# Keys and values of batches 1 to 3 loaded by heads, and a written place for every operation

## The chip, the cores and the metric

One core of a Trainium2 chip runs the kernel. The metric is the device time of one execution in microseconds; the medians are over three runs. A profiled execution leaves a trace, from which all rows below come.

## The reference

Causal attention with a memory term feeds a two-layer network; the attention's output for a token is that token's input row.

```python
# attention: B, H, S, D = 4, 8, 576, 64
scores = q @ k^T / sqrt(D), causal; a = softmax(scores)
local = a @ v
q_p = phi(q)                       # elu(q) + 1
mem_out = (q_p @ M_prev) / (q_p . z_prev + 1e-6)
g = sigmoid(beta)                  # one per head
attn = g * mem_out + (1 - g) * local
# network: 2304 tokens, 512 -> 2048 -> 512
h = x @ w_in                       # x: attn, heads side by side
y = (relu(h) + alpha * min(h, 0)) @ w_out
```

## The kernel before

**Tiling.** Each batch's 576 rows are cut into a first block of 64 and four blocks of 128. The first blocks of all four batches make a fifth set, Z, done first. Attention goes by units (batch, head, pair of blocks [1, 2] or [3, 4]); the two-layer network runs on groups of 256 tokens, in eight steps j of two 128-wide slices of the 2048. Matmuls in reduced width use pairs of f16 tiles, a high and a low part, in three products; batch 0's first pair of blocks and Z use f32.

**Tiles and phases.** `load_batch(b)` loads q, z, K (tile `kn`) and V with M_prev (tile `vn`); there is one buffer of `kn` and one of `vn`. `kn` is [partition, head, block, 64]: block i's row p of every head lies in partition p. `prep_qk` squares all of `kn` for a scale and `prep_v` takes the maximum over `vn`; `build_qk` and `build_v` split one pair of heads into f16 parts (`k<-kn`, `v<-vn`), and `build_qk` turns them by DMA transposes (`qT<-q`, `k<-k`) and copies halves (`qS<-qT`). `unit_scores` makes scores `s`, `unit_probs` the probabilities `P` and their transpose `PT<-P`, `pair_values` the products in PSUM tile `bank`, written to `xn` and transposed to `x` (`x<-xn`). `moe_in` makes `h` and `gg`, `moe_out` makes `y` and stores. At the start the weights are loaded as f64 words and converted on DVE (`to_f32`, phases C0 to C3).

**Order.** No instruction is issued while the kernel is described. `Work.add` records each with its engine, its phase name (such as `L3k` for loads of batch 3's K, `P21` for probabilities of batch 2, blocks [1, 2]) and the earlier ones whose cells it touches. `Work.issue` then gives each a rank, and `Work.lay` walks a model of the engines in time: whenever an engine is free, it takes the ready operation with the lowest rank. The order of the starts so found is the order of issue; each engine works through its own in sequence. All DMAs, loads and transposes alike, go through SP's queue. The ranks before come from three stages of `STAGES`: shifts in us by phase, or by phase and engine, added to the starts of the stage before.

Of the kernel before, what the change touches and what calls it, by code (L numbers as in the profile page):

```python
# [31 lines left out]
STAGES = [  # L32
    (2, {
        "A0": 10.6, "A:DVE": 50.6, "BK0": 102.5, "BK:ACT": -27.7, "BK:PE": 3.4, "C0": -56.4, "C1": 22.3, "C2": 335.8,
        "C3": -920, "C:ACT": 1096.2, "C:DVE": -3.8, "C:PE": -943.6, "I": -699.2, "I:DVE": 79.2, "I:POOL": 497.7,
        "J:ACT": 470.6, "J:DVE": 108, "J:PE": -179.3, "K": 47.5, "K:POOL": 2.3, "L0K": -713.8, "L0K:DMA": 228.2,
# [6 lines left out]
        "LW:DMA": 605.3, "LZ": 27.3, "LZ:DMA": -1145.9, "Lz": 8.5, "Lz:DMA": -8.6, "N": 87.9, "N:PE": 292.5,  # L43
        "P01": 4, "P03": 3.7, "P11": 777.2, "P13": 823.4, "P21": 168.1, "P23": 236.6, "P31": -675.3, "P33": -247.2,
        "P:ACT": 988.7, "P:DMA": 668.5, "P:DVE": -882.6, "P:PE": -157.8, "S0": 4737.2, "S1": -1253, "S3": -2953.6,
        "S:ACT": -87.5, "S:DVE": 168.1, "V0": -874.8, "V:DVE": 211.2, "V:PE": -90.8, "a0": 5.7, "a1": 46.8,
        "a2": -161.5, "a3": 389.6, "a4": -42.9, "a:ACT": -265.2, "a:DVE": 239.4, "bk0": -173.5, "bk1": 344.8,
        "bk2": 244.5, "bk3": 3.1, "bk:ACT": -687.5, "bk:DMA": 246.9, "bk:DVE": 1380.7, "bk:PE": 100.3, "bv0": -0.7,
# [5 lines left out]
        "o31": 144.8, "o33": 10.1, "o:ACT": -779.8, "o:DMA": 580.1, "o:DVE": -613.6, "o:PE": 33.3, "oZ": 10.8,  # L54
# [5 lines left out]
        "v:DVE": 634.9, "v:PE": 331.4, "x0": -121.5, "x:ACT": 2.1, "x:DVE": 73.7, "y0_10": -412.5, "y0_11": -68.6,  # L60
        "y0_30": 187.3, "y0_31": 1834.4, "y1_10": -18.1, "y1_11": 103.3, "y1_30": -419.6, "y1_31": 103.8,
        "y2_10": 184.2, "y2_11": 220.2, "y2_30": -3073.8, "y2_31": -122.6, "y3_10": 764.1, "y3_11": 98,
        "y3_31": 447.3, "y4_11": -1599.1, "y:ACT": -1231.1, "y:DMA": 642.8, "y:DVE": -750.7, "y:PE": 1282.7,
    }),
# [4 lines left out]
        "C3:PE": -8.9, "C:ACT": 13.2, "C:DVE": 9.3, "C:PE": -17.2, "I": -57.9, "I:POOL": -8.6, "J:ACT": -18.7,  # L69
# [6 lines left out]
        "LW3": -8.7, "LW3:DMA": -22.1, "LW:DMA": -2.8, "LZ:DMA": -42.6, "Lz:DMA": -4.4, "N": 0.9, "N:PE": -13.7,  # L76
# [5 lines left out]
        "P33:DMA": -3.8, "P33:DVE": -7.4, "P33:POOL": -37, "P:ACT": 15, "P:DMA": -20.1, "P:DVE": 8.9, "P:PE": -86.4,  # L82
# [126 lines left out]
        "y:PE": 143.8,  # L209
    }),  # L210
]
WINDOW = 3413.0
RING, SHARE = 1200, 0.95
# [36 lines left out]
class Work:  # L250
# [79 lines left out]
    def price(self, kind, name, outs, ins, kw):  # L330

        o = outs[0]
# [126 lines left out]
    def issue(self, tc):  # L459
        ops = self.ops  # L460
# [1067 lines left out]
```

## Time and profile before

| | |
|---|---|
| median of 3 runs | 563.89 us (560.77 to 564.72) |
| profiled execution | 563.66 us, span 561.9 us |
| mean granted TensorE clock | 0.982 |
| TensorE busy | 536.4 us (95%), 4421 matmuls |
| DVE busy | 450.9 us (80%) |
| ACT busy | 376.7 us (67%) |
| GpSimd busy | 82.8 us (15%) |
| DMA | 82.84 MB, 226026 packets, 216224 of them under 512 bytes |

PE is TensorE's matmul, PEld its weight load, DVE VectorE, ACT ScalarE, POOL GpSimd and SPq the queue of SyncE, on which a DMA's duration is that of its issue. Times are in us from the start of the span. [...] All instructions show line 487, the one that issues them, so groups go by tile: `out<-in`. Matmuls are pipelined and their ends are modelled, so that short gaps between them don't show.

### The profile page before, as it was taken

To read this page: it belongs to the slowest core of one execution; us is meant where nothing else is said; L and a number is where in the kernel's file an instruction comes from. 1 tells how busy PE (TensorE), PEld (TensorE's weight loads), DVE (VectorE), ACT (ScalarE), POOL (GpSimd) and SP (SyncE) were. 2 spreads that over 40 slices of the span, in tenths; PEclk is the share of its full clock that TensorE was granted. 3 is DMA by queue.
4 is the path that set the end of the run, shared out by engine and by line. 5 is a ranking of instruction groups with operands and counts; after the bars stand their busy time and mean duration, and the time that the engine had idled before them with its cause. 6 is when DMAs were issued, how large, how long until landed. Compare 5 with 4: busy or idle time off the path is not lost. (4 is left out here: it accounts for less than half of the span.)

```text
span 561.9 us, 11984 instructions
## 1 busy us (share of the span) xinstructions
PE 536.4 (95%) x4421; PEld 353.5 (63%) x4421; DVE 450.9 (80%) x1197; ACT 376.7 (67%) x790; POOL 82.8 (15%) x142
## 2 busy tenths in 40 slices
PE   9749999999999899999998999999999999999997
PEld 3448654556557566658555766578578765866663
DVE  4989999999999799999897999998679974233232
ACT  2568996778998369978785787796579873232222
POOL 3000510031220012221222110431112110000000
PEclk9869999999999999999998999999999999999999
DMA  8998595836359997579999816799446963000000
GB/s 283 239 353 202 155 238 173 244 94 153 89 127 184 214 231 170 101 140 210 194 201 198 175 34 146 160 232 178 58 118 111 167 138 88 12 11 2 37 1 37
DMA packets 226026, 82.84 MB, mean 147 GB/s; under 512 B 216224, under 2 KB 216240, under 8 KB 225968
## 3 DMA queue, kind: packets, MB, share of 16 engines
q1 hardware_dynamic: 225968, 82.09, 64.5%
q8 instruction: 34, 0.56, 0.4%
q14 instruction: 24, 0.20, 0.1%
HBM read 35.66 MB, written 5.77 MB: 74 GB/s over the span
## 5 line engine op out<-in xcount | busy, mean ns | idle before, releaser
L487 PE MATMUL h<-x,R 128*128 128x256 f16 x1536 | 246.7, 273 | 1.9 <-DMA x<-xn 1.4
L487 PE MATMUL y<-R,gg 128*128 128x512 f16 (+1 forms) x832 | 247.0, 399 | 0.8 <-ACT k L487 0.6
L487 PE MATMUL bank<-v,PT 128*128 128x64 f16 x1224 | 182.1, 193 | 5.3 <-DMA PT<-P 4.5
L487 PEld LDWEIGHTS <-R 128*128 128x128 f16 x1536 | 148.6, 98 | 36.9 <-issue 6.5
L487 PEld LDWEIGHTS <-gg 128*128 128x128 f16 x768 | 74.4, 98 | 78.3 <-DVE gg L487 1.8
L487 PEld LDWEIGHTS <-PT 128*128 128x128 f16 x1224 | 114.4, 98 | 13.6 <-DMA PT<-P 6.9
L487 POOL TENSOR_SCALAR E<-q,nrm,sm 128x64 f32<-128x64 f32 x112 | 67.9, 618 | 310.9 <-DVE sm L487 269.8
L487 ACT ACTIVATE E<-E,mx 128x320 f32<-128x320 f32 (+3 forms) x136 | 81.1, 602 | 21.5 <-DVE mx L487 17.4
L487 DVE SCALAR_TENSOR_TENSOR P<-E,mx,P 128x384 f16<-128x384 f32 (+2 forms) x112 | 75.3, 699 | 8.5 <-ACT P L487 8.4
L487 ACT ACTIVATE P<-E,mx 128x384 f16<-128x384 f32 (+2 forms) x112 | 71.0, 675 | 15.8 <-POOL E L487 12.0
L487 DVE SCALAR_TENSOR_TENSOR r<-r,oma,h 128x256 f32<-128x256 f32 x128 | 56.6, 475 | 20.2 <-ACT r L487 20.0
L487 DVE SCALAR_TENSOR_TENSOR gg<-r,gsc,gg 128x512 f16<-128x512 f32 x56 | 41.8, 748 | 36.5 <-ACT gg L487 35.0
L487 ACT ACTIVATE r<-h 128x512 f32<-128x512 f32 x72 | 42.3, 589 | 35.8 <-PE h L487 23.9
L487 ACT ACTIVATE gg<-r,gsc 128x512 f16<-128x512 f32 x56 | 40.1, 717 | 37.4 <-PE y L487 33.4
L487 DVE CUSTOM_DVE_ANT_0 E<-s,mask,pm 128x320 f32<-128x320 f32 (+2 forms) x96 | 56.9, 608 | 7.6 <-PE s L487 7.5
L487 PE MATMUL s<-k,qT 128*128 128x64 f16 (+5 forms) x136 | 37.9, 294 | 1.3 <-DMA k<-k 1.3
L487 PE MATMUL s<-k,qS 128*128 128x192 f16 (+4 forms) x120 | 34.0, 294 | 0.0
L487 PE MATMUL h<-R 128*128 128x256 f32 x128 | 32.7, 383 | 0.0
L487 PEld LDWEIGHTS h<-R 128*128 128x128 f32 x128 | 22.3, 192 | 6.6 <-issue 3.0
L487 ACT ACTIVATION_READ_ACCUMULATOR E<-E,mx 128x1 f32 x124 | 23.5, 189 | 0.0
L487 ACT ACTIVATE xn<-bank,xsc 128x256 f16<-128x256 f32 x28 | 12.9, 462 | 12.3 <-PE bank L487 12.3
L487 DVE SCALAR_TENSOR_TENSOR xn<-bank,xsc,xn 128x256 f16<-128x256 f32 x28 | 13.4, 480 | 9.4 <-ACT xn L487 9.4
(183 smaller groups left out, 636.7 us busy)
## 6 DMA issues: line engine op xcount, KB each, us to landing
q<-in_q_dram SPq DMA_DIRECT2D x16, 256.0 KB, 4.3
vn<-in_v_dram SPq DMA_DIRECT2D x16, 256.0 KB, 5.2
out_dram<-t SPq DMA_DIRECT2D x16, 256.0 KB, 2.4
kn<-in_moe_w_in_dram SPq DMA_DIRECT2D x6, 512.0 KB, 6.7
kn<-in_moe_w_out_dram SPq DMA_DIRECT2D x6, 512.0 KB, 5.3
kn<-in_k_dram SPq DMA_DIRECT2D x12, 256.0 KB, 4.0
qS<-qT SPq DMA_DIRECT2D x24, 128.0 KB, 2.6
R<-in_moe_w_in_dram SPq DMA_DIRECT2D x4, 512.0 KB, 5.6
```

The costliest lines, as they stand in the source:

```text
L487: fn(*a, **kw)
```

## The change

In batches 1 to 3, K's four blocks of 128 rows were loaded by four DMAs, each with all heads (256 KB), and so were V's. Now each of the eight heads has one DMA that fills its four blocks (128 KB). The loads of the first 64 rows and of M_prev stay as they were, and so does batch 0.

`STAGES` and the code that applies it are gone. A table `PLAN` has for each phase and engine the places of its operations in the order in which they are recorded, in steps of 0.1 us, each written as the difference from the one before (`"L3k:DMA": "3792 -1014 -243 ..."` stands for 379.2, 277.8, 253.5 us and so on). One walk of `lay` with these places as ranks gives the order. The prices of DMAs in the walk's model are changed as well; they act on nothing but the order. The first place of `L3k` and of `L3v` belongs to the load of the first 64 rows, the second of `L3v` to M_prev, the other eight to the heads; `Lz` holds four loads of z, then alpha and beta; `LZ` and `LK` load q and K of the set Z.

```diff
-STAGES = [
-    (2, {
...
-]
+PLAN = {
...
+    "C0:DVE": "266 -71 175 -199 -45 66 272 16 -42 -2 -88 -168 195 509 53 -247",
...
+    "L2k:DMA": "1613 310 59 137 -18 -348 366 -10 -351",
...
+    "L2v:DMA": "2338 -399 291 -329 120 -56 -356 365 -45 -341",
...
+    "L3k:DMA": "3792 -1014 -243 -4 8 3 27 94 108",
...
+    "L3v:DMA": "2368 50 -173 128 -104 -158 160 162 -185 19",
...
+    "LK:DMA": "-81 -3 99 44",
...
+    "LW0:DMA": "-536 -16 156 -6 -106 -66 7 27",
...
+    "LZ:DMA": "-4 -36 52 47",
...
+    "Lz:DMA": "81 -42 49 56 -75 -35",
...
+    "P21:DMA": "2538 31 75 213 -255 1050 -92 55",
...
+    "a4:DVE": "-426 248 -21 522",
...
+}
...
         if kind == "DMA":
             kb = n * o.shape[0] * size / 1024
             if "transpose" in name:
-                return (800 + 1.75 * kb if kb > 400 else 1130 + 0.6 * kb), 190 + 3.45 * kb, 1655, -1
+                return (800 + 1.75 * kb, 4.1 * kb, 1700, -1) if kb > 400 else (1130 + 0.6 * kb, 3.78 * kb, 1885, -1)
             run = min(x.ap[-1][1] * (2 if x.dtype == F16 else 4) for x in (o, ins[0]))
             packets = 1024 * kb / min(run, 4096)
             if run < 256:
-                return 500, 0.45 * packets, 1800, packets
+                return 500, 0.45 * packets, 2000, packets
             if run >= 4096:
-                return 400, (2.75 if self.phase in ("LW0", "LW1") else 4.9) * kb, 2000, packets
+                rate, late = {"LW0": (3.2, 2600), "LW1": (2.7, 2450)}.get(self.phase, (3.55, 2150))
+                return 400, rate * kb, late, packets
             if run >= 512:
-                return 540, max(300, 4.06 * kb), 1800, packets
-            return 620, (273 if kb > 200 else 200) + 4.17 * kb, 2100, packets
+                if o.tensor.name in self.fixed:
+                    return 400, 1.4 * kb, 1950, packets
+                return (560, 5.3 * kb, 1765, packets) if kb < 200 else (530, 4 * kb, 1800, packets)
+            return (600, 4.5 * kb, 2050, packets) if kb > 200 else (620, 6 * kb, 2090, packets)
...
-        late = [0.0] * len(ops)
-        hold = [max(op[5], op[8][0]) for op in ops]
-        pe = 0.0
-        for i in reversed(range(len(ops))):
-            took = ops[i][8][0] + ops[i][8][1] if ops[i][0] == "DMA" else hold[i]
-            late[i] = min([late[f] - lag for f, lag in after[i]], default=0.0) - took
-            if ops[i][6]:
-                late[i] = pe = min(late[i], pe - hold[i])
-        rank = late
-        for passes, bias in STAGES:
-            rank = [x + 1e3 * sum(bias.get(k, 0) for k in dict.fromkeys((
-                op[7], op[7].rstrip("0123456789_") + ":" + op[0], op[7] + ":" + op[0]))) for x, op in zip(rank, ops)]
-            for n in range(passes):
-                if n:
-                    back = self.lay(after, before, [-s - h for s, h in zip(start, hold)], True)
-                    rank = [-s - h for s, h in zip(back, hold)]
-                start = self.lay(before, after, rank)
-            rank = start
+        plan = {}
+        for x, steps in PLAN.items():
+            at, ranks = 0, []
+            for step, _, times in (y.partition("*") for y in steps.split()):
+                for _ in range(int(times or 1)):
+                    at += int(step)
+                    ranks.append(100.0 * at)
+            plan[x] = iter(ranks)
+        start = self.lay(before, after, [next(plan[f"{op[7]}:{op[0]}"]) for op in ops])
...
         if b:
+
+            def heads(dst, src):
+                return [(dst[:, h, 1:NS], src[b, h, 64:, :].rearrange("(i p) d -> p i d", p=128)) for h in range(H)]
+
+            todo[1][1:] = heads(kn, k)
+            todo[2][2:] = heads(vn, v)
             todo = [[lambda o=o, i=i, c=c: load(o, i, f"L{b}{c}") for o, i in t] for t, c in zip(todo, "qkv")]
         else:
```

## Rows read from the trace of the kernel before

**Rows 1.** Stages of the span: busy us (instructions) by engine, clock, DMA.
```profile
0.00:20.00 20.00, 18.57 (x74) 7.96 (x74) 12.09 (x25) 5.28 (x9) 4.28 (x13) 1.00 0.96 281
20.00:40.00 20.00, 9.98 (x84) 7.54 (x85) 18.17 (x79) 13.96 (x48) 0.00 (x0) 0.69 1.15 304
...
140.00:260.00 120.00, 116.09 (x1043) 77.44 (x1042) 114.66 (x294) 96.86 (x195) 19.39 (x32) 1.00 0.74 160
260.00:325.00 65.00, 60.35 (x558) 40.71 (x557) 56.88 (x164) 47.23 (x108) 14.46 (x22) 0.97 0.95 187
325.00:555.00 230.00, 229.41 (x2090) 156.69 (x2089) 151.66 (x388) 133.97 (x267) 28.29 (x50) 1.00 0.44 91
...
sum 561.90, PE 536.37 PEld 353.48 DVE 450.91 ACT 376.67 POOL 82.79; mean PE 67.05 PEld 44.19 DVE 56.36 ACT 47.08 POOL 10.35
```

**Rows 2.** Who waited for whom, TensorE, whole span: us, times, longest.
```profile
PE bank L487 <- DMA PT<-P: 4.5, 5, 2.7
PE bank L487 <- DVE stv L487: 3.5, 1, 3.5
```

**Rows 3.** The same, from 260 to 325 us.
```profile
PE bank L487 <- DMA PT<-P: 4.3, 4, 2.7
PE s L487 <- DMA k<-k: 0.4, 1, 0.4
```

**Rows 4.** Timeline, TensorE: start, us, instruction, [idle before it, releaser].
```profile
302.77 0.20 PE L487 MATMUL bank<-v,PT 128*128 128x64 f16 x1 [2.65 <-DMA PT<-P]
```

**Rows 5.** Timeline, SP's queue, from 292 to 312 us.
```profile
292.94 1.16 SPq L487 DMA_DIRECT2D q<-in_q_dram  x2
294.14 2.07 SPq L487 DMA_DIRECT2D kn<-in_k_dram  x2
296.32 5.59 SPq L487 DMA_TRANSPOSE PT<-P  x2
301.97 1.29 SPq L487 DMA_DIRECT2D kn<-in_k_dram  x2
...
305.00 0.68 SPq L487 DMA_DIRECT2D vn<-in_v_dram  x1
...
307.91 3.22 SPq L487 DMA_DIRECT2D vn<-in_v_dram  x4
```

**Rows 6.** Instructions on the tile PT, whole span.
```profile
DMA to landing us min/median/max: 2.9/3.9/6.4
```

**Rows 7.** Instructions on the tile PT, from 293 to 306 us.
```profile
DMA to landing us min/median/max: 3.3/4.8/6.4
```

**Rows 8.** Stages after the stall, columns as in rows 1.
```profile
304.00:306.00 2.00, 2.00 (x10) 0.93 (x8) 0.97 (x4) 0.50 (x2) 0.00 (x0) 0.52 1.24 278
306.00:308.00 2.00, 2.00 (x7) 0.78 (x6) 1.86 (x7) 1.54 (x5) 0.00 (x0) 0.62 0.63 142
```

**Rows 9.** Timeline, DVE: splits of K and V, batches 2 and 3.
```profile
270.56 0.87 DVE L487 SCALAR_TENSOR_TENSOR k<-kn,scr,k 128x640 f16<-128x640 f32 x1
...
299.98 0.74 DVE L487 SCALAR_TENSOR_TENSOR v<-vn,scr,v 128x512 f16<-128x512 f32 x1
...
364.28 0.87 DVE L487 SCALAR_TENSOR_TENSOR k<-kn,scr,k 128x640 f16<-128x640 f32 x1
```

**Rows 10.** Timeline, TensorE, where batch 1 takes over.
```profile
185.86 3.11 PE L487 MATMUL h<-x,R 128*128 128x256 f16 x27 [1.21 <-DMA x<-xn]
...
195.26 0.33 PE L487 MATMUL s<-k,qT 128*128 128x192 f16 x2 [0.94 <-DMA k<-k]
```

**Rows 11.** Timeline, SP's queue, start.
```profile
3.99 2.52 SPq L487 DMA_DIRECT2D q<-in_z_prev_dram  x4
...
12.06 0.66 SPq L487 DMA_DIRECT2D q<-in_q_dram  x1
```

**Rows 12.** Timeline, DVE, start.
```profile
20.35 1.23 DVE L487 SCALAR_TENSOR_TENSOR R<-E,R 128x1024 int32<-128x1024 int32 x1
21.50 0.68 DVE L487 TENSOR_REDUCE stq<-q 128x1 f32<-128x512 f32 x1
```

More of the change, by code (lines that the diff above doesn't have):

```diff
@@ L29 @@
 PN = [1, 1, 1, 1, 1]
-STAGES = [
-    (2, {
-        "A0": 10.6, "A:DVE": 50.6, "BK0": 102.5, "BK:ACT": -27.7, "BK:PE": 3.4, "C0": -56.4, "C1": 22.3, "C2": 335.8,
-        "C3": -920, "C:ACT": 1096.2, "C:DVE": -3.8, "C:PE": -943.6, "I": -699.2, "I:DVE": 79.2, "I:POOL": 497.7,
-        "J:ACT": 470.6, "J:DVE": 108, "J:PE": -179.3, "K": 47.5, "K:POOL": 2.3, "L0K": -713.8, "L0K:DMA": 228.2,
[6 rows of a table removed]
[L43 to L48, printed above, removed]
[5 rows of a table removed]
-        "o31": 144.8, "o33": 10.1, "o:ACT": -779.8, "o:DMA": 580.1, "o:DVE": -613.6, "o:PE": 33.3, "oZ": 10.8,
[5 rows of a table removed]
[L60 to L64, printed above, removed]
[4 rows of a table removed]
-        "C3:PE": -8.9, "C:ACT": 13.2, "C:DVE": 9.3, "C:PE": -17.2, "I": -57.9, "I:POOL": -8.6, "J:ACT": -18.7,
[6 rows of a table removed]
-        "LW3": -8.7, "LW3:DMA": -22.1, "LW:DMA": -2.8, "LZ:DMA": -42.6, "Lz:DMA": -4.4, "N": 0.9, "N:PE": -13.7,
[5 rows of a table removed]
-        "P33:DMA": -3.8, "P33:DVE": -7.4, "P33:POOL": -37, "P:ACT": 15, "P:DMA": -20.1, "P:DVE": 8.9, "P:PE": -86.4,
[21 rows of a table removed]
-        "h4_11:PE": -16.7, "h:ACT": 10, "h:DVE": 8.9, "h:PE": -16.3, "n": -27.5, "n:PE": -9.4, "o01": -15,
[5 rows of a table removed]
-        "o33:DVE": 21.3, "o33:PE": -55.2, "o:ACT": -0.5, "o:DMA": -50.1, "o:DVE": 13.1, "o:PE": -18, "oZ": -97,
[4 rows of a table removed]
-        "q:ACT": 39, "q:DVE": 9.7, "r0:ACT": 0.9, "r0:DVE": 9.9, "r:ACT": 35.7, "r:DVE": 13.6, "s01:ACT": -1.2,
[4 rows of a table removed]
-        "s33:ACT": 1.7, "s33:PE": -49.1, "s:ACT": 12.1, "s:DVE": 8.9, "s:PE": -16.3, "sZ": 8.1, "sZ:ACT": 98.3,
[14 rows of a table removed]
-        "y4_11:PE": -16, "y:ACT": 21.9, "y:DMA": 2.5, "y:DVE": 8.4, "y:PE": -16.3,
-    }),
[4 rows of a table removed]
-        "C3:PE": -26.7, "C:ACT": 47.4, "C:DVE": -22.5, "C:PE": 1, "I:DVE": -32.9, "I:POOL": 4.3, "J": 37.8,
[13 rows of a table removed]
-        "P33:DMA": -13.2, "P33:DVE": -9.1, "P:DMA": -3.5, "P:DVE": -22.3, "P:PE": 0.2, "P:POOL": -11, "S0": 2.9,
[27 rows of a table removed]
-        "o33:PE": 65.8, "o:ACT": 7.4, "o:DMA": -10.7, "o:DVE": -24.8, "o:PE": 144.2, "oZ": -53.6, "oZ:ACT": 8.9,
[9 rows of a table removed]
-        "s33:DVE": -8.2, "s33:PE": 41.6, "s:ACT": -5, "s:DVE": -22.3, "s:PE": 143.8, "sZ": -0.9, "sZ:ACT": 37.5,
[15 rows of a table removed]
-        "y:PE": 143.8,
-    }),
-]
```

562 rows, old and new, of tables (PLAN, STAGES) are left out of this document.

## Prediction

> **What bounds the kernel now.** I read the span cut into stages first, then TensorE's waits, then single instructions around the longest wait. TensorE is busy for 536.37 us of 561.9 [rows 1], so the time can only fall where it idles or runs at the lower clock, and the cut shows where that is. From 325 to 555 us it is busy for 229.41 of 230 us at full clock: nothing is to be had there, whatever the order. From 20 to 40 us it is busy for only 9.98 of 20 us at a granted clock of 0.69. From 140 to 260 us it idles 120 - 116.09 = 3.91 us, from 260 to 325 us 65 - 60.35 = 4.65 us, and the clock of that stage is 0.97. The list of waits says on what: 4.5 us on transposes of the probabilities (PT<-P), which go through SP's queue, 4.3 us of them between 260 and 325 us; the 3.5 us on stv belong to the start [rows 2, 3].
>
> The one stall worth the name ends at 302.77 us: TensorE had waited 2.65 us for a PT tile before its next bank matmul [rows 4]. On SP's queue two q loads and two K loads of batch 3, 1 MB in four DMAs, went out from 292.94 to 296.2 us, and the two PT<-P transposes behind them held SP for 5.59 us [rows 5]. Over the whole kernel a PT tile lands 3.9 us after its issue in the median [rows 6]; of the two issued here one took 6.4 us, the longest of all 56 [rows 7]. The loads ahead cost that transpose 2.5 us, which is the stall. [...]
>
> **The change part by part.** *Removed: four block loads each of K and V for batches 1 to 3, with what they tie together.* A block holds all eight heads, so it may overwrite its slice of kn (or vn), of which there is one buffer, only when the last head pair of the batch before has been split. A head load needs only its own pair. In the trace batch 2's K is split from 270.56 us on and the last of its V until 300.7 [rows 9]; the loads of batch 3 go out from 294.14 to 311.1 [rows 5]. By heads the first K load could leave at 271.5. The new places ask for it: V's pieces of batch 3 stand at 211 to 243 us, K's eight heads at 253 to 278, the PT transposes of batch 2's first half at 254 to 365, so SP takes each piece soon after its pair is free, a few at a time instead of four together. I take the 302 us stall as gone with its clock, 2.65 + 1.72 = 4.4 us, and half of the stage's other waits on transposes (4.3 - 2.65 on PT<-P and 0.4 on k<-k [rows 3], 2.05 together): 1.0. **Term A: -5.4 us**, bounds 0 and -6.4 (4.3 + 0.4 + 1.7).
>
> Where batch 1 takes over, TensorE waits 1.21 us for x<-xn and 0.94 us for k<-k [rows 10]. No K or V load is in flight then; the order of transposes causes it, which the new places also change. **Term B: half, -1.1 us**, bounds 0 and -2.15.
>
> *Added: pieces.* Per batch 16 loads of 128 KB take the place of 8 of 256 KB; bytes and the runs of 256 bytes stay the same. SP is held 0.68 us by a 128 KB load, and 2.07, 1.29 and 3.22 us by the eight large ones [rows 5]: 16 x 0.68 = 10.9 against 6.6, 4.3 us more per batch, 13 us in three. Nobody waits for the loads themselves: the first split of batch 3's K starts at 364.28 us [rows 9]. What hides the 13 us is SP's slack between transposes; one that stands behind a piece is late by 0.68 us. Bounds 0 and +13; I take one piece ahead of one awaited transpose in each batch, nearest to the row of a single load: **term C: +2.0 us**.
>
> [...]
>
> *Moved: everything, by the new table.* The three stages of shifts by phase give way to a place for each operation; the list scheduler takes, of the operations that are ready, the one with the lowest place. One move is certain from the table alone, since these loads wait for nothing: at the start the loads of z, K and Q of the first rows are re-ranked. Before, four z loads leave from 3.99 us and Q's first at 12.06 [rows 11]. Now K stands at -8.4 to 5.9, Q at -4 to 5.9, z at 3.9 to 14.4. z is 4 x 128 KB = 0.52 MB, at the 281 GB/s of the first 20 us [rows 1] 1.9 us of transfer. DVE's first operation on q starts at 21.50 us, behind conversions of weights of 1.23 us each [rows 12], and the waits on stv and on what follows hang on that chain. **Term D: -2.0 us** (z's 1.9, rounded). Bounds: 0, because DVE is busy 18.17 of the 20 us from 20 to 40 [rows 1], and if its whole work and not its order sets when the h matmuls can go, the gain is nil; and -4.4, with the last two conversions (2 x 1.23 us) put behind q as well. From 325 us on: 0, for want of idle time; should the new order starve TensorE, that is in the rivals.
>
> **Sum.** -5.4 - 1.1 + 2.0 - 2.0 = -6.5. The profiled execution took 563.66 us (span 561.9), 0.23 below the median 563.89, a difference that I leave out. Forecast 557.2 us, 1.2% below the median.
>
> **Rivals.** *Larger.* The new places fit the whole order better, not only the loads: every idle microsecond of 140 to 325 us goes (3.91 + 4.65) with the 1.7 of the clock, and half of the 10.0 idle from 20 to 40 us. For it: those are waits of order, with DVE and ACT not full in the stage 260 to 325 (56.88 and 47.23 of 65). Against it: in the first 40 us DVE is nearly full. 563.66 - 15.3 = 548.4 us.
>
> *No change.* Stalls move: K pieces that leave from 271 us meet the batch's own k<-k transposes, for which TensorE waits already, and the earlier start is eaten by DVE's conversions. A and B come to nothing, C and D cancel: 563.7 us.
>
> *Slower.* The pieces stand below most transposes in the table, so a run of them leaves as soon as buffers come free and holds SP for up to 4.3 us longer than the blocks did; the PT<-P behind is late by that, TensorE, which takes its matmuls in order, stalls, and the clock falls as it did after 302 us. In two of three batches: 563.66 - 2.0 + 2 x (4.3 + 1.7) = 573.7 us. It decides from where a transpose that TensorE needs next has more than the 1 MB of rows 5 ahead of it. Against it: heads come free by pairs, one split after another, so pieces come in twos.
>
> [...]
>
> **How the numbers follow.** Chances: forecast 0.41, larger 0.18, no change 0.25, slower 0.15, serial 0.01. A measurement of this kernel tells about 1% from no change, 5.6 us. The forecast case lies below 558.2 in three quarters (0.31) and above it in the rest (0.10); larger is all faster; no change is all same; slower and serial are slower. Hence faster 0.49, same 0.35, slower 0.16. Range: from 547, just below the larger case, to 568, which takes in no change and the milder part of the slower cases, leaving out some 0.05 below and 0.13 above.
>
> **What would show it.** Right: no wait on PT<-P over 1 us between 260 and 325 us and a granted clock of 1.00 there; K and V loads of batch 3 leaving in twos between the splits; Q's first load ahead of z's on SP, and DVE's first stq before 20 us; the stage from 325 us as full as now. Wrong: a run of head loads of 5 us or more directly ahead of a PT<-P, followed by a wait of TensorE and a dip of the clock; or new waits on k<-k and x<-xn in the half after 325 us, where the new order can only lose.

## The result, and the profile after

The changed kernel takes **569.62 us** (median of 4 runs, 569.07 to 571.19) where before takes 564.08 (4 runs beside them): a ratio of 1.012, 95% interval 1.0083 to 1.0156. Timed again beside the experiments it came to 1.0136 (1.0111 to 1.0161). It is slower by 1.2 to 1.4%; the forecast was 557.2 us, with a range up to 568.

The stages of the profiled execution of the changed kernel (569.07 us, span 567.3), columns as in rows 1 (bounds and length in us; busy us and instructions of PE, PEld, DVE, ACT and POOL; TensorE's granted clock, 1.00 being full speed; the mean busy share of the 16 DMA engines; the GB/s that they moved):

```profile
20.00:40.00 20.00, 7.68 (x81) 5.97 (x81) 18.02 (x86) 14.62 (x49) 0.00 (x0) 0.60 0.90 251
120.00:140.00 20.00, 18.53 (x90) 9.04 (x89) 19.30 (x53) 14.43 (x22) 3.25 (x4) 0.91 0.52 112
140.00:260.00 120.00, 115.29 (x1023) 75.27 (x1022) 112.31 (x287) 95.09 (x188) 20.16 (x33) 1.00 0.70 153
260.00:325.00 65.00, 63.10 (x625) 45.27 (x624) 60.82 (x167) 49.12 (x109) 14.70 (x22) 1.00 1.04 208
325.00:555.00 230.00, 226.50 (x2077) 155.06 (x2076) 153.37 (x392) 135.60 (x275) 24.22 (x52) 1.00 0.42 91
...
126.00:128.00 2.00, 2.00 (x4) 0.73 (x4) 2.00 (x6) 2.00 (x4) 0.00 (x0) 0.55 0.88 199
128.00:130.00 2.00, 2.00 (x5) 0.51 (x5) 2.00 (x2) 1.41 (x3) 0.00 (x0) 0.59 0.92 150
```

Against [rows 1]: from 260 to 325 us TensorE idles 1.90 us where it idled 4.65, and the granted clock is 1.00 where it was 0.97. That is the gain that was forecast. It is lost elsewhere, most of it in stages that were full: from 325 to 555 us TensorE idles 3.50 us (0.59 before), and from 120 to 140 us it idles 1.47 and then works at a granted clock of 0.55 and 0.59. The stage from 20 to 40 us, which was not full, loses too: TensorE is busy for 7.68 us where it was for 9.98, so it idles 2.3 us more. The bounds are times and not places in the work, so a stage of one kernel holds a little other work than that of the other. From 120 to 140 us the kernel before was full:

```profile
120.00:140.00 20.00, 20.00 (x141) 11.26 (x140) 19.94 (x51) 16.02 (x25) 2.05 (x5) 1.00 0.58 130
```

TensorE's waits in four stages of the changed kernel in turn (120 to 140, 140 to 260, 260 to 325, 325 to 470 us). Left out are the shorter ones of the second and the last, and in the second one on xn of 0.8, which is there before as well:

```profile
PE bank L729 <- ACT kn L729: 1.5, 1, 1.5
...
PE h L729 <- DVE r L729: 0.8, 3, 0.4
PE y L729 <- DVE t L729: 0.7, 2, 0.5
PE bank L729 <- DMA PT<-P: 0.7, 1, 0.7
PE h L729 <- DMA x<-xn: 0.7, 1, 0.7
...
PE s L729 <- DVE tt L729: 0.9, 1, 0.9
PE h L729 <- DMA x<-xn: 0.6, 1, 0.6
PE bank L729 <- DMA PT<-P: 0.4, 1, 0.4
...
PE s L729 <- DVE mx L729: 1.2, 2, 0.7
PE y L729 <- ACT gg L729: 1.2, 1, 1.2
PE h L729 <- DMA x<-xn: 0.8, 1, 0.8
```

The reader is to see that the releasers have changed. Before, TensorE waited for transposes on SP's queue [rows 2, 3, 10]; of the 4.3 us on PT from 260 to 325 us, 0.4 are left, and k<-k is gone at batch 1. In their place stand waits of 0.2 to 1.5 us on tiles that VectorE and ScalarE write (kn, r, t, tt, mx, gg), most of them where before there was none. A second execution of the same sequence (changed_again, below) idles much the same in each stage, 12.27 us from 20 to 40, 1.47 from 120 to 140, 4.52 from 140 to 260, 2.23 from 260 to 325 and 3.59 from 325 to 555 us. Its single small waits differ, though: from 260 to 325 us it waits 1.1 us on k<-k and none on tt. The sums repeat, a single small wait need not. Landings did not get quicker: a PT tile lands after 2.9/4.0/6.6 us (least, median, longest) where [rows 6] had 2.9/3.9/6.4.

**The stall at 123 us, followed back.** Timeline of the changed kernel, lines of DVE, POOL, ACT and PE:

```profile
113.12 1.21 DVE L729 SCALAR_TENSOR_TENSOR R<-q,R 128x1024 int32<-128x1024 int32 x1
...
117.84 0.88 DVE L729 SCALAR_TENSOR_TENSOR P<-E,mx,P 128x640 f16<-128x640 f32 x1 [1.78 <-ACT P L729]
...
123.02 0.68 DVE L729 SCALAR_TENSOR_TENSOR R<-kn,R 128x512 int32<-128x512 int32 x1
...
113.38 3.62 POOL L729 TENSOR_SCALAR E<-q,nrm,sm 128x64 f32<-128x64 f32 x4 [35.94 <-DVE sm L729]
...
116.28 1.44 ACT L729 ACTIVATE P<-E,mx 128x512 f16<-128x512 f32 x2 [3.04 <-POOL E L729]
...
123.74 1.06 ACT L729 ACTIVATE kn<-R 128x1024 f32<-128x1024 f32 x1 [1.80 <-DVE R L729]
...
124.94 0.39 PE L729 MATMUL bank<-wsq,ones 128*128 128x4 f32 x2 [1.47 <-ACT kn L729]
```

Read from the bottom: TensorE waits for ScalarE's kn, ScalarE for the last R<-kn,R of a weight conversion on VectorE, and VectorE had stood idle for 1.78 us with the rest of that conversion ready, because the instruction at the head of its queue, P<-E,mx,P, waited for ScalarE, and that for GpSimd. Neither the P ahead of the conversion nor a slow GpSimd is new: the order of before has such P there as well and VectorE waits 0.51 us for ScalarE at one of them (116.54 us), and GpSimd's four instructions on E take 4.19 us there where they take 3.62 now (the first of them alone is longer now, 2.33 us against 1.30). The same two places before, on ScalarE and on TensorE:

```profile
123.02 1.04 ACT L487 ACTIVATE kn<-R 128x1024 f32<-128x1024 f32 x1
...
124.79 0.28 PE L487 MATMUL bank<-wsq,ones 128*128 128x4 f32 x2
```

ScalarE's kn came 0.72 us earlier, and TensorE took the matmul on wsq at almost the same time, 124.79 us, without idling before it, because it had other matmuls ahead of it until then. In the new order it stands at that matmul from 123.47 us on. So the stall has two sides, each a matter of order: the operand comes later, and TensorE asks for it sooner.

**The start.** The changed kernel's SP and DVE, against [rows 11, 12]:

```profile
8.95 6.87 SPq L729 DMA_DIRECT2D q<-in_q_dram  x3
...
18.54 0.63 SPq L729 DMA_DIRECT2D q<-in_z_prev_dram  x1
...
19.68 0.68 DVE L729 TENSOR_REDUCE stq<-q 128x1 f32<-128x512 f32 x1
```

Q's first load goes out at 8.95 instead of 12.06 us and VectorE's first stq comes at 19.68 instead of 21.50, as forecast. It bought nothing: TensorE's wait for stv is 4.1 us where it was 3.5 [rows 2]. Ahead of it TensorE now waits 3.21 us for ScalarE's k, where it waited 3.15 in four shorter waits. Two more waits follow, 1.14 us on scd and 0.91 on ScalarE's q. With the longer one on stv these two are what the stage from 20 to 40 us lost, to within half a microsecond:

```profile
22.58 1.15 PE L729 MATMUL s<-q,k 128*64 128x64 f32 x32 [3.21 <-ACT k L729]
27.31 0.58 PE L729 MATMUL bank<-scd,ones 1*128 1x1 f32 x2 [1.14 <-DVE scd L729]
```

### The profile page after: what moved, and what is told of

It reads as the page before. It is cut to its first block, busy times and chain, and to the rows that moved or that the text cites. A ratio compares the mean times of both kernels' runs of the same rounds, so it can differ in the third digit from the quotient of the medians.

```text
span 567.3 us, 12027 instructions
## 1 busy us (share of the span) xinstructions
PE 535.6 (94%) x4421; PEld 352.6 (62%) x4421; DVE 452.2 (80%) x1197; ACT 376.9 (66%) x790; POOL 81.5 (14%) x142
## 4 chain that ended last, share of the span: by engine, by line
PE 54%; DVE 17%; DMA 12%; ACT 7%; issue 5%; SPq 4%; POOL 2%; ACTq 0%; DVEq 0%; POOLq 0%
PE y L729 22%; PE h L729 21%; DMA PT<-P 5%; PE s L729 5%; PE bank L729 4%; SPq L729 4%; DVE P L729 3%; DVE E L729 3%; DVE r L729 2%; DVE R L729 2%; ACT P L729 2%; POOL E L729 2%; DMA out_dram<-t 1%; DMA x<-xn 1%; DMA R<-in_moe_w_in_dram 1%
## 5 line engine op out<-in xcount | busy, mean ns | idle before, releaser
L729 PE MATMUL y<-R,gg 128*128 128x512 f16 (+1 forms) x832 | 251.2, 398 | 2.8 <-ACT gg L729 1.8
L729 POOL TENSOR_SCALAR E<-q,nrm,sm 128x64 f32<-128x64 f32 x112 | 65.4, 597 | 331.4 <-DVE sm L729 215.7
L729 DVE SCALAR_TENSOR_TENSOR P<-E,mx,P 128x640 f16<-128x640 f32 (+3 forms) x112 | 75.6, 699 | 11.9 <-ACT P L729 11.7
L729 ACT ACTIVATE P<-E,mx 128x640 f16<-128x640 f32 (+3 forms) x112 | 70.4, 673 | 18.8 <-POOL E L729 14.6
L729 DVE CUSTOM_DVE_ANT_0 E<-s,mask,pm 128x576 f32<-128x576 f32 (+3 forms) x96 | 56.1, 608 | 5.5 <-PE s L729 5.2
L729 PE MATMUL s<-k,qT 128*128 128x192 f16 (+5 forms) x136 | 37.2, 294 | 2.1 <-DVE mx L729 1.2
L729 PE MATMUL s<-k,qS 128*128 128x192 f16 (+4 forms) x120 | 32.6, 294 | 0.0
```

The source lines that it names most:

```text
L729: fn(*a, **kw)
```

## The experiments

Every kernel below issues a written-out sequence, made from the two orders of issue (their instructions show line 383 in the rows below, the line that issues them):

```diff
         with tc.manual_schedule():
-            for i in sorted(range(len(ops)), key=lambda i: (start[i], i)):
+            for i in ORDER:
```

Theory 1: the new order costs the time, in small waits at the heads of the engines' queues. Theory 2: the 24 more DMAs do. The pieces are the loads by heads, the blocks those of all heads. Each ratio is to the kernel before, timed beside it on the same chip.

| run | median us | before | ratio, 95% interval |
|---|---|---|---|
| changed_again | 569.74 | 561.73 | 1.0136 (1.0111 to 1.0161) |
| pieces_only | 562.79 | 562.21 | 1.0010 (0.9992 to 1.0028) |
| early_pieces | 569.94 | 562.21 | 1.0115 (1.0095 to 1.0136) |
| blocks_in_new_order | 577.97 | 562.21 | 1.0262 (1.0239 to 1.0285) |
| middle_part | 561.48 | 562.21 | 0.9979 (0.9964 to 0.9993) |
| old_until_140 | 566.64 | 562.01 | 1.0084 (1.0055 to 1.0112) |
| old_until_260 | 563.19 | 562.01 | 1.0020 (1.0000 to 1.0040) |
| new_until_325 | 566.86 | 562.01 | 1.0110 (1.0073 to 1.0148) |
| splits_first | 567.42 | 562.01 | 1.0112 (1.0084 to 1.0140) |
| two_repairs | 568.68 | 562.56 | 1.0120 (1.0089 to 1.0150) |
| loads_behind | 563.38 | 561.73 | 1.0016 (0.9997 to 1.0035) |
| transposes_first | 563.73 | 562.56 | 1.0020 (1.0005 to 1.0035) |
| row_sum_later | 563.46 | 562.79 | 1.0023 (1.0002 to 1.0043) |
| z_later | 564.09 | 561.73 | 1.0042 (1.0028 to 1.0055) |

### Loads or order

```diff
 # pieces_only
-ORDER = before        # load of block n of K or V
+ORDER = before        # loads of heads 2n and 2n+1 in its place
```

> The order of the kernel before, operation by operation; only the loads of K and V of batches 1 to 3 are by heads, two heads where one block stood. Theory 1 (the re-ordering of all other work costs the time, the loads by heads cost little): within 1% of before, some 564 to 566 us, with the wait for PT at 302 us still there, since two heads stand where a block stood. Theory 2 (24 more DMAs on SP's queue cost the time): most of the 5.5 us is here already, 568 to 571 us.

Measured 1.0010, with 1 inside the interval: theory 2 falls. The pieces do cost SP time: it is held 3.02 + 2.28 us by batch 3's K and 4.43 by its V, 9.73 us against the 6.6 of the blocks [rows 5], and nobody waits for that. The wait on PT at 302 us is still there:

```profile
293.99 3.02 SPq L383 DMA_DIRECT2D kn<-in_k_dram  x4
...
301.27 2.28 SPq L383 DMA_DIRECT2D kn<-in_k_dram  x4
...
307.86 4.43 SPq L383 DMA_DIRECT2D vn<-in_v_dram  x8
...
302.07 0.20 PE L383 MATMUL bank<-v,PT 128*128 128x64 f16 x1 [2.35 <-DMA PT<-P]
```

```diff
 # blocks_in_new_order
-ORDER = changed       # loads of heads
+ORDER = changed       # the four block loads of K or V where its last head stood
```

> The order of the changed kernel, operation by operation; only the loads of K and V of batches 1 to 3 are by blocks of rows again, the four blocks where the last of the heads stood. Theory 1: as slow as the changed kernel or slower, 569 to 574 us, since the order of everything else is kept and the four blocks now leave together. Theory 2: back at 564 us.

Measured 1.0262, 1.3% above the changed kernel. The loads by heads are thus not the cost; in the new order they save some 7 us (1.0262 less 1.0136, of 562) against blocks that wait for the last head. Blocks at a better place of that order were not tried.

```diff
 # early_pieces: pieces_only, and in batches 2 and 3
-ORDER = [..., last use of the head's place, other work, load of the head, ...]
+ORDER = [..., last use of the head's place, load of the head, ...]
```

> As the kernel with the loads by heads in the order of before, and each head load of batches 2 and 3 is moved up to right behind the step that frees its place in kn or vn. Theory 1: the load comes away from the two PT transposes, the wait at 302 us goes with its low clock, 4.4 us by the prediction's rows: 559 to 562 us. Theory 2: no faster than the loads by heads alone, 568 us or more, with SP's queue held by pieces ahead of transposes.

Measured 1.0115: here theory 1's forecast was wrong, by its sign. The "slower" rival of the prediction is what happened, at another transpose. TensorE's longest wait from 140 to 220 us, and three stages behind it:

```profile
PE s L383 <- DMA k<-k: 4.3, 1, 4.3
```

```profile
198.00:200.00 2.00, 1.47 (x8) 1.06 (x8) 0.63 (x1) 1.49 (x3) 0.00 (x0) 0.50 1.07 227
200.00:202.00 2.00, 2.00 (x7) 0.76 (x6) 2.00 (x6) 0.56 (x1) 0.00 (x0) 0.50 0.95 235
202.00:204.00 2.00, 2.00 (x7) 0.78 (x6) 0.58 (x1) 0.36 (x1) 0.00 (x0) 0.50 0.62 167
```

The wait for k<-k where batch 1 takes over, 0.94 us before [rows 10], is 4.3 with batch 2's pieces on SP's queue ahead: SP issues these k<-k at 194.53 us, in pieces_only at 190.56. And the granted clock is 0.50 for six microseconds behind the wait. Pieces that leave as soon as they may are not better than blocks here.

### In which stage

```diff
 # old_until_140, old_until_260: before's sequence up to 140 (260) us, then the rest as in changed
 # new_until_325: changed's up to 325 us, then the rest as in before
 # middle_part: before's up to 260, changed's up to 325, then the rest as in before
+ORDER = merge((before, 260), (changed, 325), (before, end))
```

> Loads by heads. The order of before up to what its trace shows at 140 us, then the order of the changed kernel for the rest. Theory 1 (the new order loses in stages of its own, one wait at a time): the waits of the changed kernel up to 140 us are gone, among them 1.47 us at 123 us and the low clock behind it, and those after 140 us stay: 4 to 5 us faster than the changed kernel, 564 to 566 us. Theory 3 (one early loss is carried through and the rest would run as well as before): 561 us or less, as the orders' better middle would then count in full.

> Loads by heads. The order of before up to what its trace shows at 260 us, then the order of the changed kernel. Theory 1: the gain from 260 to 325 us is there, the waits of the new order after 325 us too (1.2 us on gg at 381, 0.8 on x at 415, 0.7 on mx at 459): 561 to 564 us. Theory 3: 558 us, as if the end were without cost.

> Loads by heads. The order of the changed kernel up to what its trace shows at 325 us, then the order of before. Theory 1: all but what the new order loses after 325 us, some 3 us: 565 to 567 us. Theory 3: as slow as the changed kernel, 569 to 570 us, since the loss was early.

> Loads by heads. The order of before up to what the trace of before shows at 260 us, then the order of the changed kernel up to what its trace shows at 325 us, then the order of before for all that is left. Theory 1, with the gain and the loss of the new order in different stages: the stage from 260 to 325 us keeps the gain of 4 to 5 us and the stages around it lose nothing: 558 to 561 us. Theory 2: the pieces are all in, so 566 us or more.

Differences of the ratios, from pieces_only to changed_again, of 562 us: the loads alone 1.0010, +0.6 us; new order from 260 to 325 us (middle_part less pieces_only) -1.7; after 325 us (old_until_260 less middle_part) +2.3; from 140 to 260 us +3.6; up to 140 us +2.9. They add up to 7.6 us, the 1.36% of the changed kernel, as they must; by the intervals each is known to 1 to 2 us, and each merged sequence has a seam that neither kernel has. The two figures with old_until_140 are the weakest: its ten runs spread from 563.2 to 570.7 us, and the profiled one is the fastest of them, so that its trace doesn't show what the others lost. Theory 3 (one early loss is carried through to the end) falls with old_until_140, which is 0.84% slower than before although its start is that of before. middle_part is faster than both kernels, than the kernel before by 0.2%; against pieces_only it gains 1.7 us, less than the 4 to 5 us expected. TensorE's waits in it from 260 to 325 us show why: PT is down from pieces_only's 3.9 us to 0.6, but it waits 2.6 us on k, gg and x, where pieces_only waits 0.7 on k and x. new_until_325 agrees with the sum: 1.0136 less 0.41% is 1.0095, inside its interval.

```profile
PE s L383 <- DMA k<-k: 1.1, 1, 1.1
PE y L383 <- ACT gg L383: 0.9, 1, 0.9
PE h L383 <- DMA x<-xn: 0.6, 1, 0.6
PE bank L383 <- DMA PT<-P: 0.6, 1, 0.6
```

### Two waits of the new order taken out

```diff
 # splits_first: VectorE's queue in the changed kernel
+R<-kn,R  R<-kn,R  R<-kn
 P<-E,mx,P
-R<-kn,R
 P<-E,mx,P  P<-E,mx,P  str<-stq
-R<-kn,R
 stv<-vn
-R<-kn
```

> The changed kernel; on VectorE alone three instructions of a weight conversion (two R<-kn,R and one R<-kn) go ahead of the P<-E,mx,P at 117.84 us that waits 1.78 us for GpSimd and ScalarE. If that in-order wait makes the stall of TensorE at 123 us (1.47 us on kn) and the low clock from 126 to 130 us (0.55 and 0.59, 2 x 0.45 + 2 x 0.41 = 1.7 us), both go: 3 us faster than the changed kernel, 566 to 567 us. If VectorE's own load and not its order makes it, the stall stays or comes a little later: 569 to 570 us.

The stall and its clock are gone from the trace (stages as above, 0.55 and 0.59 before the repair):

```profile
126.00:128.00 2.00, 2.00 (x9) 0.70 (x8) 2.00 (x4) 2.00 (x5) 0.00 (x0) 1.00 1.00 224
128.00:130.00 2.00, 2.00 (x10) 0.81 (x7) 2.00 (x2) 1.17 (x2) 0.00 (x0) 1.00 0.81 163
```

So with three instructions at another place that stall does not arise, and VectorE's load is not its cause. In time it shows as 1.0112 beside 1.0136, 1.3 us of the 3 expected, and the intervals overlap: the mechanism is shown, its worth is not. The traces suggest where some of the gain goes: from 140 to 260 us TensorE idles 5.91 us here and 6.24 in two_repairs, 4.71 and 4.52 in the two executions of the changed kernel's order.

```diff
 # two_repairs: splits_first, and on ScalarE at 380 us
+r<-h  gg<-r,gsc
 P<-E,mx  P<-E,mx
-r<-h  gg<-r,gsc
```

> The changed kernel with two of its in-order waits taken out: on VectorE the three instructions of a weight conversion ahead of P<-E,mx,P, as in the run before; and on ScalarE r<-h and gg<-r ahead of the two P<-E that at 379.86 us wait 1.25 us until a PT<-P transpose has read P. Theory 1 (the new order loses by instructions that wait at the head of an engine's queue while TensorE's next operand stands behind them): the waits on kn at 123 us and on gg at 381 us (1.16 us) are both gone and none takes their place, 3.2 us by the wait of 1.47, the low clock of 1.7 and 1.16, less what is hidden: 565 to 567 us where the changed kernel has 569.7. Rival (each wait that is taken out comes back at the next operand, as in the run with the loads behind the transposes): 568 to 570 us.

Measured 1.0120, not to be told from splits_first. The wait on ScalarE's gg (1.2 us in the stage from 325 us) is gone, and one on VectorE's gg stands in its place, since VectorE's own P<-E,mx,P waits at the head of that queue:

```profile
PE y L383 <- DVE gg L383: 1.6, 1, 1.6
...
380.45 1.55 DVE L383 SCALAR_TENSOR_TENSOR P<-E,mx,P 128x640 f16<-128x640 f32 x2 [1.74 <-ACT P L383]
```

The rival was right for this wait: it came back at the next operand. The one on kn did not; 0.2 us of it is left in both repaired kernels.

### The stall at 302 us of the old order

```diff
 # loads_behind: SP's queue in pieces_only, from 293 us
+PT<-P  PT<-P
 q  q  K0 K1 K2 K3
-PT<-P  PT<-P
 K4 K5 K6 K7  x<-xn
 # transposes_first
 PT<-P  PT<-P  K0 K1 K2 K3
+x<-xn
 q  q  K4 K5 K6 K7
-x<-xn
 # row_sum_later: transposes_first, and on VectorE
-stv<-vn  (with the copy and the scaling of its result)
 some 20 instructions: P<-E,mx,P, r<-r,oma,h, ...
+stv<-vn
```

> Loads by heads in the order of before, and on SP's queue alone two q loads and four K loads of batch 3 go behind the two PT<-P transposes that they stood ahead of at 293 us. The prediction's account of the stall at 302 us (loads ahead of the transposes, term A): the wait for PT and the low clock behind it go, 4.4 us by its rows: 558 to 560 us. Against it: the transposes are late for another reason, or the loads now hold the next transpose: 562 us, with a wait for x or PT a little later.

> Loads by heads in the order of before, and on SP's queue alone: the two PT<-P transposes of 297 us first, then four K loads, then the x<-xn transpose, then two q and four K loads. The K loads no longer stand eight in a row ahead of x<-xn, which took 5.26 us there. If the waits at 300 us come from the loads that stand directly ahead of an awaited transpose: neither the 2.4 us on PT nor the 2.5 us on x comes, 559 to 561 us, and faster than both kernels. If SP's queue as a whole is too full from 290 to 315 us: a wait of 1 to 2.5 us on the next transpose, 562 to 563 us.

> As the run with the transposes first, and on VectorE stv<-vn with the two small instructions behind it stands some 20 instructions later. It waited 4.40 us at the head of VectorE's queue until 309.38 us for the row of V and M_prev that SP had sent off at 306, with r<-r,oma,h behind it, for which TensorE then waited 3.57 us. Theory 1 (the stall at 300 us of the order of before has three ends in a row, PT, x and this one, and only the last that is left sets the time): with all three gone TensorE runs through from 295 to 315 us, 4 us less: 558 to 560 us, faster than both kernels. Rival (SP's queue is too full there, a fourth wait follows on the PT transposes of 306.8 or 312.9 us, behind eight V loads): 562 to 563 us.

None of the three is faster than pieces_only. The wait moves, and each trace shows where. TensorE in loads_behind, VectorE and TensorE in transposes_first, SP, ScalarE and TensorE in row_sum_later:

```profile
306.96 0.27 PE L383 MATMUL h<-x,R 128*128 128x256 f16 x1 [2.48 <-DMA x<-xn]
```

```profile
309.38 0.69 DVE L383 TENSOR_REDUCE stv<-vn 128x1 f32<-128x512 f32 x1 [4.40 <-DMA vn<-in_M_prev_dram]
...
312.82 0.39 PE L383 MATMUL h<-x,R 128*128 128x256 f16 x1 [3.57 <-DVE r L383]
```

```profile
306.50 1.60 SPq L383 DMA_TRANSPOSE PT<-P  x1
...
310.12 0.62 ACT L383 ACTIVATE P<-E,mx 128x384 f16<-128x384 f32 x1 [3.59 <-DMA PT<-P]
...
314.35 5.01 PE L383 MATMUL h<-x,R 128*128 128x256 f16 x29 [2.97 <-ACT t L383]
```

2.35 us on PT at 302, then 2.48 on x at 307, then 3.57 on r at 313 behind the row of V and M_prev, then 2.97 at 314 behind ScalarE, whose P waits for the PT<-P that SP issues at 306.50. All of it has SP's queue of 293 to 313 us in front of it, 1 MB of K, 1 MB of V and q beside the transposes. Which wait stands last changed with the order; in all four orders one of 2.35 us or more stood there. The rival of row_sum_later was right, at the transpose of 306.50 us. Of the orders tried only the new one, which moves everything in that stretch (middle_part), is rid of it; that SP's queue is too full for any change within it was not shown.

### The start

```diff
 # z_later: SP's queue in pieces_only
 w_in x5  alpha
-z z z z
 w_in  beta  w_in  w_in  q K q q K V q K K
+z z z z
```

> Loads by heads in the order of before, and on SP's queue alone the four z loads go from the front to behind the first loads of K and Q. Term D of the prediction: the start is shorter by the transfer of z, 560 to 561 us. Against it: VectorE's whole work in the first 40 us sets when TensorE can go on, and the order of the loads gives nothing: 562 to 563 us.

Measured 1.0042 against 1.0010: slower, by 1.8 us. The first rows are TensorE's longest wait up to 120 us in z_later and a wait of VectorE there; the last is TensorE's longest wait in pieces_only:

```profile
PE bank L383 <- DVE stv L383: 4.8, 1, 4.8
...
24.34 0.69 DVE L383 TENSOR_TENSOR t<-q,q 128x512 f32<-128x512 f32 x1 [1.54 <-DMA q<-in_z_prev_dram]
```

```profile
PE bank L383 <- DVE stv L383: 3.5, 1, 3.5
```

In pieces_only VectorE has no such wait for z. In z_later it stands for 1.54 us at an instruction that reads z, with stv behind it in its queue: the first stv starts at 28.47 us, in pieces_only at 26.87. This too is a wait at the head of a queue.

## Why the prediction was wrong

**The step that failed** is the one on what is moved: "From 325 us on: 0, for want of idle time; should the new order starve TensorE, that is in the rivals". A stage without idle time was read as one where nothing could happen; it is one where a new order can only lose, as the prediction's last lines say and its sum does not. The same zero stood, unsaid, for 40 to 140 us. Measured: +2.3 us after 325 (2.9 us more idle by the stages), +2.9 up to 140. By the stages that last figure should be larger, 2.7 us more idle up to 40 us, 1.1 from 40 to 120 and 1.47 at 123 us, with 0.41 x 2 + 0.45 x 2 = 1.7 of clock behind it; since the runs give 2.9 to within 2 us, how much each of these is worth stays open. The step reaches further than its zero. For all that the new order does outside the stage of term A the forecast has -3.1 us (B, D and the zeros), and the sequences give +8.8 (2.9 + 3.6 + 2.3). That is 11.9 of the 14.1 us between the forecast -6.5 and the +7.6 measured beside the experiments; term A's size makes 3.7, and C gives 1.4 back. The "slower" rival looked for the loss on SP's queue and found a price there, but most of the waits that came stand on VectorE's and ScalarE's queues (kn, r, t, tt, mx, gg above), and no row of before could have shown them. That such waits make up the loss is read from the traces; it was tested at the two places of the repairs and at z. What could have been read from before is the risk: every operation placed anew, 2090 matmuls of them in the 230 us in which TensorE idled 0.59 [rows 1].

**Term A** (-5.4): the mechanism held as far as the forecast went, the wait on PT is 0.4 us instead of 4.3 and the clock 1.00, and by the stages 2.75 us of idle and 0.03 x 65 = 1.95 of clock came back, 4.7. In time the stage is worth 1.7 us (middle_part less pieces_only), since k, gg and x wait 2.6 us in it, and since the trace of pieces_only has no low clock to give back. Its cause was taken too narrowly. In the changed kernel four K pieces and two q loads still stand ahead of two PT<-P (from 286.31 to 290.62 us on SP, with one copy of q between them), one of them still takes 6.6 us, and TensorE waits for PT 0.4 us in the whole stage. So loads ahead of a late transpose are not enough for the stall; what TensorE has to do meanwhile counts as well. And with the loads put behind the transposes the stall moved on three times. Part of its price, the 1.7 us of clock, does not always come with the stall either: in the trace, behind the 2.35 us of pieces_only the granted clock stays at 1.00 from 304 to 308 us, where [rows 8] had 0.52 and 0.62, from which the forecast's 1.72 us are estimated (2 x 0.48 + 2 x 0.38).

**Term B** (-1.1): wrong in sign. The wait for k<-k is gone and that for x is 0.7 instead of 1.21, but r, t, gg and PT took their place; the stage idles 4.71 us instead of 3.91. The sequences say 3.6 us for 140 to 260 us. That is more than the 0.8 of idle time; the changed kernel also gets 1023 TensorE instructions into these 120 us where before had 1043, and how much of the rest is the uncertainty of two ratios, known to 1.9 us, stays open.

**Term C** (+2.0): the mechanism was right, the size small. SP is held 3.1 us longer per batch (4.3 forecast) and the loads alone cost 0.6 us, with zero inside the interval. The 0.01 for the serial case, a piece that holds SP's queue until it has landed, falls with the eight V pieces that leave SP within 4.43 us, one every 0.55 us: in the changed kernel the loads on vn from 290 to 320 us land 2.4 us after their issue or later. Half the size cost at most some 1.6 us in time (1.0028), with nobody waiting for these loads; what it does to their bandwidth no run here measures.

**Term D** (-2.0): wrong in sign. The 1.9 us of z's transfer were taken for time that the path gets back, but z is itself on the path to the stv that TensorE waits for, through VectorE's queue: z behind K and Q makes that wait 1.3 us longer, and the time 1.8.

Of the signs to look for, Q's early load, stq before 20 us, the clock of 1.00 and the short waits on PT came; the K and V pieces left in ones to fours rather than twos. The stage from 325 us is less full, which was the sign of an error.

So -5.4 - 1.1 + 2.0 - 2.0 became -1.7 + 3.6 + 0.6 + 2.9 + 2.3, where D is within the 2.9 of the first 140 us.

## What to carry to other kernels

A stage whose bounding engine is full is not a zero in the sum of a new order but a risk to one side, here 2.3 us; ask of each operation that moves which engine holds it at the head of its queue, and what stands behind it there. A wait that is named by its releaser is a place in a queue: before a gain is booked for its removal, look which operand is late next, and whether the queue as a whole is full in that stretch. And a written order is best taken over stage by stage, each timed alone: here only one stage in four was better than what it replaced. Ask the same of the engine that waits: the stall at 123 us has TensorE's own new order behind it as well as VectorE's.

## What the hardware showed that was not expected

GpSimd's instructions on E differ in length, from 0.39 to 2.78 us for one shape. Instructions of POOL on the tile E, changed kernel, whole span and from 112 to 118 us (least, median, longest ns):

```profile
L729 POOL TENSOR_SCALAR E<-q,nrm,sm x112: 390/397/2775, 113.4 to 482.3; 128x64 f32<-128x64 f32 x112
...
L729 POOL TENSOR_SCALAR E<-q,nrm,sm x4: 393/472/2332, 113.4 to 116.6; 128x64 f32<-128x64 f32 x4
```

One of the four at 113.38 us, which the stall at 123 us goes back to, took 2.33 us where the median of 112 is 0.40, and lay beside VectorE's two R<-q,R of 1.21 us each. The last two of the four, which ran from 116.23 us on while VectorE idled (its 1.78 us up to 117.84), took 0.77 us together. That VectorE's instructions stretch GpSimd's agrees with the trace at this place, but is not shown: no run here takes them away. The stretch is not the changed kernel's: before, the longest of the same four took 1.99 us.

A stall of TensorE is not always followed by the low clock. In the profiled executions, behind 2.65 us of idling the granted clock fell to 0.52 [rows 4, 8], behind 2.35 us at the same place (pieces_only) it stayed at 1.00, and behind 1.47 us at 123 us of the changed kernel it fell to 0.55.
